# A state-space scan and a gated feed-forward layer on one core: first weights held, x on another queue, decay rows loaded once

## The chip, the cores and the metric

The kernel runs on one core of one Trainium2 chip. A core has a matrix engine (TensorE, PE in the profile), VectorE (DVE), ScalarE (ACT), GpSimd (POOL), SyncE (SP, which here only issues DMA transfers) and 16 DMA engines. Each engine works through its own instructions in order and waits on semaphores that other engines and transfers raise. The metric is the device time of one execution in microseconds (us); lower is better.

## The reference

Inputs: x (4 batches, 8 heads, 768 steps, 32 values), decay a (4, 8, 768), B and C (4, 8, 768, 16), all fp32, and two weight matrices in float64, w_in (256 x 2048) and w_out (2048 x 256). The first part is a Mamba-2 scan in chunks of 32 steps:

```python
log_a = np.log(np.clip(a, 1e-06, 1.0))
...
    cum = np.cumsum(la, axis=-1)
    L = np.exp(cum[:, :, :, None] - cum[:, :, None, :]) * causal
    y_intra = np.einsum('bhij,bhjd->bhid', (C_c @ B_c.T) * L, xc)
    y_inter = np.einsum('bhin,bhnd->bhid', Cc, state) * exp(cum)
    state = decay_full * state + sum over j of B_j x_j exp(cum_last - cum_j)
...
h = y @ w_in                 # y as (3072, 256)
g = h * (1.0 / (1.0 + np.exp(-1.702 * h)))
out = g @ w_out
```

(the middle lines are shortened; an einsum over heads and chunks is meant). The result is (3072, 256) fp32.

## The kernel before, in words

**Tiling.** The 768 steps are cut into NC = 6 chunks of 128, each of two halves of 64 steps. A group g holds one chunk of all four batches, 512 tokens; it has two pairs p of two batches each (PG = 2). For each group the scan gives yT (256 x 512), `hidden(g, f)` makes 16 blocks f of 128 hidden units from w_in, and a projection from w_out adds them up. For group 0 the products are plain (`hidden`, `project_all`); from group 1 on they use mixed operands with seven products for eight (`first`, `product`), which make up most of the span.

**Weights.** The float64 weights are fetched as 32-bit words in ten pieces (`PIECES`): 0 to 3 are 0.5 MB of w_in each (two blocks f), 4 and 5 are 1 MB of w_in each (four blocks), 6 to 9 are 1 MB of w_out each. `fetch(i)` issues the two transfers of piece i (line 175), on SyncE. Four buffers hold them, pieces 0 and 1 sharing one and 2 and 3 another, so pieces 6 to 9 are fetched when `join` of an earlier piece is done. With `held=True`, VectorE first writes one column of the target (line 166); since VectorE works in order, this holds the transfer, and all behind it on SyncE, until VectorE has come to that place.

A piece becomes fp32 in steps: `fields(i)` takes exponent and mantissa bits on VectorE (lines 188 and 191), `clamp(i)` does two Relu steps on ScalarE (200 and 202), `rounded(i)` adds the low word (206), `join(i)` sets the sign and multiplies (220 and 226), writing w_in or w_out. `narrow(i)` is rounded(i), fields(i+1), join(i), so join(i) stands behind the wait for piece i+1.

**The start.** Chunk 0 is done in its own way. a of chunk 0 (az0, four copies of 32 rows), C and B are loaded; VectorE turns C and B (`turn_blocks`, line 541); TensorE builds decay exponents in PSUM (493, 499, 488), ScalarE takes their exponential (529). GpSimd copies the decays to the ends (`drop_of`, 452) and scales C by the decay (`since_start`, 583). TensorE computes the scores C B (`score`, 597), VectorE multiplies the decays by them (`weigh`, 608) and B by the drops (`ends_first`, 458). `finish` multiplies by x (`intra`, 724) and by the state (`inter`, 709); `gain` (628) and `keep_first` (644) make the state; ScalarE copies yT (736). `pads` and `dense` are matmuls of ones with no use for the result, which fill places where TensorE would wait. Then `hidden(0, f)` runs for f = 0 to 15 (786), with other work hung in between by `at`.

**Queues around the change.** SyncE issues, in order: az0, half of C, part of B, piece 0, piece 1 (held until the first weighing), pieces 2 to 5 (held until after the ends), az, piece 6 and what follows. GpSimd issues the rest of B, builds `pick`, and issues x of pairs 0 and 1 (line 145) before its drops. az is all 768 steps of a, 32 rows written four times over into 128 partitions (line 1088); `clip` limits it on VectorE (361, 363) in `store_a`, which writes it to a DRAM scratch (1118); `pick_a` multiplies chunk 1 of it into operands on ScalarE (372).

`in_order` fixes the order of every engine's instructions to the program's.

## Time and profile before

| what | us |
|---|---|
| device time, three runs | 351.01, 353.86, 354.13; median 353.86 |
| profiled execution, device time | 352.01 |
| profiled execution, span | 350.3 |
| TensorE busy | 341.9 |
| VectorE busy | 255.8 |
| ScalarE busy | 149.5 |
| GpSimd busy | 40.7 |
| first block of `hidden(0, f)` starts | 17.42 |
| projection of group 0 starts | 49.0 |

The granted TensorE clock is full in every slice. The span runs from the first to the last instruction; the device time has 1.7 us around it. In the views, times are from the start of the span, "L608" is a line of the kernel, "x12" the number of instructions, and what stands in brackets is how long the engine was idle before and what ended that. Busy TensorE time is modelled from the starts of its instructions. DMA issues appear under the queue of their engine (SPq, POOL); the length there is that of issuing, not of the transfer.

### The profile page before, as it was taken

To read this page: it belongs to the slowest core of one execution; us is meant where nothing else is said; L and a number is where in the kernel's file an instruction comes from. 1 tells how busy PE (TensorE), PEld (TensorE's weight loads), DVE (VectorE), ACT (ScalarE), POOL (GpSimd) and SP (SyncE) were. 2 spreads that over 40 slices of the span, in tenths; PEclk is the share of its full clock that TensorE was granted. 3 is DMA by queue.
4 is the path that set the end of the run, shared out by engine and by line. 5 is a ranking of instruction groups with operands and counts; after the bars stand their busy time and mean duration, and the time that the engine had idled before them with its cause. 6 is when DMAs were issued, how large, how long until landed. Compare 5 with 4: busy or idle time off the path is not lost.

```text
span 350.3 us, 8534 instructions
## 1 busy us (share of the span) xinstructions
PE 341.9 (98%) x3514; PEld 281.1 (80%) x3514; DVE 255.8 (73%) x476; ACT 149.5 (43%) x333; POOL 40.7 (12%) x78
## 2 busy tenths in 40 slices
PE   8897999999999999999999999999999999999996
PEld 6666874545688888888888888888888888899996
DVE  7787999999789988749986557986454654455463
ACT  6767774005254322743442444433554321554320
POOL 8305500300297000000000000000000000000000
PEclk9999999999999999999999999999999999999999
DMA  5699986533529000466122326120000120000221
GB/s 136 187 296 253 279 180 148 87 72 59 94 57 189 2 0 5 74 129 100 23 35 60 52 78 120 21 33 9 0 4 2 17 33 12 1 2 0 33 31 60
DMA packets 82784, 26.02 MB, mean 74 GB/s; under 512 B 68841, under 2 KB 81001, under 8 KB 82745
## 3 DMA queue, kind: packets, MB, share of 16 engines
q1 hardware_dynamic: 79864, 23.41, 32.0%
q0 software_dynamic: 1888, 1.74, 2.2%
q8 instruction: 27, 0.44, 0.5%
q10 hardware_dynamic: 992, 0.33, 0.4%
q14 instruction: 13, 0.10, 0.1%
HBM read 22.22 MB, written 3.24 MB: 73 GB/s over the span
## 4 chain that ended last, share of the span: by engine, by line
PE 79%; DVE 8%; DMA 6%; POOL 3%; SPq 2%; issue 1%; ACT 1%; POOLq 0%; DVEq 0%
PE acc L944 28%; PE X L842 19%; PE Y L852 14%; PE acc L951 7%; DMA bits<-in_moe_w_out_dram 4%; PE y L724 3%; PE h L786 2%; PE y L709 2%; PE o L884 2%; DVE p L220 2%; SPq L269 1%; PE cb L597 1%; DMA a<-scratch 1%; DVE m L206 1%; DVE L L608 1%
## 5 line engine op out<-in xcount | busy, mean ns | idle before, releaser
L847 ACT ACTIVATE ac<-X 128x256 f32<-128x256 f32 x76 | 29.0, 382 | 80.0 <-PE X L842 79.6
L944 PE MATMUL acc<-mg,mw 128*128 128x256 f32 x192 | 54.5, 379 | 0.0
L971 DVE TENSOR_TENSOR gT<-Y,ac 128x512 f32<-128x512 f32 x38 | 26.2, 690 | 37.2 <-PE Y L852 33.9
L819 ACT ACTIVATE gT<-gT 128x512 f32<-128x512 f32 (+1 forms) x76 | 39.3, 519 | 31.7 <-DVE gT L971 31.1
L842 PE MATMUL X<-my,mi 128*128 128x256 f32 x152 | 45.1, 379 | 0.0
L971 DVE TENSOR_TENSOR gT<-Y,b 128x256 f32<-128x256 f32 x38 | 15.8, 418 | 34.0 <-PE Y L852 34.0
L944 PEld LDWEIGHTS acc<-mg,mw 128*128 128x128 f32 x192 | 36.5, 190 | 5.0
L786 PE MATMUL h<-yT,w_in 128*128 128x128 f32 (+2 forms) x182 | 36.3, 357 | 2.0 <-DVE w_in L226 1.8
L944 PE MATMUL acc<-gT,w_out 128*128 128x256 f32 x128 | 35.5, 379 | 0.0
L786 PEld LDWEIGHTS h<-yT,w_in 128*128 128x128 f32 x182 | 26.8, 191 | 10.3 <-issue 5.6
L842 PEld LDWEIGHTS X<-my,mi 128*128 128x128 f32 x152 | 28.0, 190 | 3.7
L884 PE MATMUL o<-gT,w_out 128*128 128x512 f32 x64 | 28.6, 597 | 0.0
L810 DVE TENSOR_TENSOR mg<-gT 128x512 f32<-128x512 f32 x40 | 27.2, 680 | 0.0
L944 PEld LDWEIGHTS acc<-gT,w_out 128*128 128x128 f32 x128 | 24.2, 190 | 3.4 <-ACT yT L759 0.2
L847 ACT ACTIVATE b<-X 128x256 f32<-128x256 f32 x38 | 14.6, 383 | 20.4 <-PE X L842 20.0
L842 PE MATMUL X<-yT,w_in 128*128 128x256 f32 x76 | 23.2, 389 | 0.0
L852 PE MATMUL Y<-yT,w_in 128*128 128x256 f32 x76 | 22.7, 381 | 0.0
L852 PE MATMUL Y<-my,mi 128*128 128x256 f32 x76 | 22.6, 379 | 0.0
L842 PE MATMUL X<-my,w_in 128*128 128x256 f32 x76 | 22.6, 381 | 0.0
L852 PE MATMUL Y<-yT,mi 128*128 128x256 f32 x76 | 22.5, 379 | 0.0
L884 PEld LDWEIGHTS o<-gT,w_out 128*128 128x128 f32 x64 | 11.8, 190 | 13.2 <-issue 12.7
L387 DVE TENSOR_TENSOR_SCAN L<-a,idents 128x1024 f32<-128x1024 f32 x9 | 20.5, 2274 | 0.0
(140 smaller groups left out, 569.3 us busy)
## 6 DMA issues: line engine op xcount, KB each, us to landing
a<-scratch SPq DMA_DIRECT2D x18, 256.0 KB
bits<-in_moe_w_out_dram SPq DMA_DIRECT2D x8, 512.0 KB
x<-in_x_dram SPq DMA_DIRECT2D x20, 128.0 KB
bits<-in_moe_w_in_dram SPq DMA_DIRECT2D x8, 256.0 KB
bits<-in_moe_w_in_dram SPq DMA_DIRECT2D x4, 512.0 KB
out_dram<-ob SPq DMA_DIRECT2D x128, 16.0 KB
af<-in_a_dram SPq DMA_DIRECT2D x20, 64.0 KB
zC<-in_C_dram SPq DMA_DIRECT2D x36, 32.0 KB
```

The costliest lines, as they stand in the source:

```text
L387: nc.vector.tensor_tensor_scan(out=L, data0=ra[p].rearrange("p k e -> p (k e)"), data1=idents.rearrange("p h i -> p (h i)"), initial=0.0, ...
L724: nc.tensor.matmul(out=y[i][t][D * q:D * q + D, 2 * n + k], lhsT=rx[p][side, k, h], rhs=L[side, k, h // Q, h % Q], start=begin(i, t, (q,)) ...
L786: nc.tensor.matmul(out=h[:, cols], lhsT=w_in[:, f, k], rhs=yT[g][:, k, cols], start=(k == 0 and e == 0), stop=(k == NK - 1), skip_group_ch ...
L810: nc.vector.tensor_tensor(out=t[:, 0:2], in0=B[:, :, 1], in1=B[:, 0], op=ALU.subtract)
L819: nc.scalar.activation(o, i, AF.Silu, scale=GELU_SCALE)
L842: nc.tensor.matmul(out=s["X"], lhsT=lhsT, rhs=rhs, start=i == "1", stop=i == "4", skip_group_check=True)
L847: nc.scalar.activation(copy, s["X"], AF.Copy)
L852: nc.tensor.matmul(out=o, lhsT=lhsT, rhs=rhs, start=s.pop("new", False), stop=i != "5", skip_group_check=True)
L884: nc.tensor.matmul(out=o[c], lhsT=w_out[:, c, f], rhs=gT[g, f // 2][:, f % 2], start=(f == 0), stop=(f == NF - 1), skip_group_check=True)
L944: nc.tensor.matmul(out=acc[g][0][i], lhsT=w, rhs=h, start=(j == 0 and (i, 0) in begins), stop=(j == NF // 2 - 1), skip_group_check=True)
L951: nc.tensor.matmul(out=o[k] if type(o) is list else o[:, cols], lhsT=h[:, cols], rhs=w, start=(j == 0 and (i, k) in begins), stop=(j == NF ...
L971: nc.vector.tensor_tensor(out=o, in0=v, in1=w, op=ALU.add)
```

## The change

Piece 0 is fetched after the turn of C, held by VectorE's memset, and x of both pairs follows it on SyncE instead of GpSimd. fields(0) (both steps) and clamp(0) come before the first weighing. a is loaded in two parts behind piece 1: chunk 1 in four copies (az1), and all chunks once, in 32 partitions (az); GpSimd clips both. One `dense` is left out and one comes a group earlier; there is one more pad.

```diff
-    az = ffn.tile([P, 4 * TG // 2], FP32, tag="mg", name="az", bufs=3)[:, :NC * P].rearrange(
+    az = ffn.tile([P, 4 * TG // 2], FP32, tag="mg", name="az", bufs=3)[:NB * NH, :NC * P].rearrange(
         "p (c s) -> p c s", c=NC)
+    az1 = const.tile([P, 1, P], FP32, name="az1")
...
     load_blocks(0, "B", [nc.gpsimd, nc.sync, nc.gpsimd, nc.sync, nc.gpsimd, nc.sync, nc.gpsimd, nc.gpsimd])
-    fetch(0)
...
-    for p in range(PG):
-        load(p, "x", nc.gpsimd)
...
     def clip(t):
 
-        nc.vector.tensor_scalar(out=t, in0=t, scalar1=1e-6, scalar2=1.0,
+        nc.gpsimd.tensor_scalar(out=t, in0=t, scalar1=1e-6, scalar2=1.0,
                                 op0=ALU.max, op1=ALU.min)
-        nc.vector.memset(t.rearrange(by_chunk, s=2)[:, :, :, 0], 0.0)
+        nc.gpsimd.memset(t.rearrange(by_chunk, s=2)[:, :, :, 0], 0.0)
...
         c, b = place(p)
+        assert c == 1
...
-                nc.scalar.activation(X[:, k, q], az[:, c], AF.Copy, scale=pick[:, b + k, q:q + 1])
+                nc.scalar.activation(X[:, k, q], az1[:, 0], AF.Copy, scale=pick[:, b + k, q:q + 1])
...
-                if p == 0 and (k, t) == (0, 1):
+                if p == 0 and (k, t) == (1, 0):
                     dense(begun_y["banks"][0][:, 2 * P:])
...
-            dense(begun_y["banks"][0][:, 2 * P:])
             intra(1, pairs[1])
...
-    pads(30, busy)
+    pads(31, busy)
...
     differ_of(0)
     turn_blocks(0, "C")
+    fetch(0, held=True)
+    for p in range(PG):
+        load(p, "x")
     mask_blocks(1)
...
     fold_ident(1)
+    fields(0)
+    clamp(0)
     weigh(0, (slice(0, 1),))
     fetch(1, held=True)
+    rows = a.rearrange("b h s -> (b h) s")
+    nc.sync.dma_start(out=az1[:, 0], in_=rows[:, P:2 * P].unsqueeze(0).to_broadcast([R, NB * NH, P]))
+    nc.sync.dma_start(out=az.rearrange("p c s -> p (c s)"), in_=rows)
+    for t in az1, az:
+        clip(t)
     weigh(0, (slice(1, 2),))
...
     for i in range(2, 6):
         fetch(i, held=i == 2)
-    nc.sync.dma_start(out=az.rearrange("p c s -> p (c s)"), in_=a.rearrange(
-        "b h s -> (b h) s").unsqueeze(0).to_broadcast([R, NB * NH, NC * P]))
-    fields(0, (0,))
     for k in range(2):
         weigh(1, (slice(k, k + 1),))
-    fields(0, (1,))
     rounded(0)
     finish(range(PG), (0,))
     gain(range(PG), (0,))
-    clamp(0)
     keep_first(0)
...
     def store_a():
-        clip(az)
         for i, side in enumerate(SIDES):
-            nc.sync.dma_start(out=scratch[:, i].rearrange("c r i -> r c i"), in_=az[:32, :, side])
+            nc.sync.dma_start(out=scratch[:, i].rearrange("c r i -> r c i"), in_=az[:, :, side])
```

## The prediction

> **What bounds the kernel now.** I read the page first, then the waits of the first 100 us, then the timeline of that part, then the DMA rows.

> The page: totals, and busy tenths in 40 slices of 8.76 us.

> ```profile
> span 350.3 us, 8534 instructions
> ...
> PE 341.9 (98%) x3514; PEld 281.1 (80%) x3514; DVE 255.8 (73%) x476; ACT 149.5 (43%) x333; POOL 40.7 (12%) x78
> ...
> PE   8897999999999999999999999999999999999996
> ...
> DVE  7787999999789988749986557986454654455463
> ...
> DMA  5699986533529000466122326120000120000221
> ```

> TensorE is the bound from slice 6 on: nothing the change touches can be gained there. What can move lies in the first four slices, where TensorE shows 8 and 7, and at places where it waits. Waits of 0 to 100 us (total, times, longest):

> ```profile
> DVE p L188 <- DMA bits<-in_moe_w_in_dram: 2.8, 2, 2.0
> ...
> PE h L786 <- DVE w_in L226: 1.8, 1, 1.8
> ...
> PE y L709 <- DVE L L608: 0.8, 1, 0.8
> DVE p L188 <- DMA bits<-in_moe_w_out_dram: 0.8, 1, 0.8
> ```

> So TensorE loses 1.8 us once to weights and 0.8 us once to a weighing, and VectorE waits on arriving weights. Timeline of 28 to 60 us (start, length, engine, line; idle before and its releaser):

> ```profile
> 31.31 0.69 DVE L188 TENSOR_SCALAR p<-bits 128x1024 uint32<-128x1024 uint32 x1 [2.00 <-DMA bits<-in_moe_w_in_dram]
> ...
> 34.08 3.69 PE L786 MATMUL h<-yT,w_in 128*128 128x256 f32 x16 [1.82 <-DVE w_in L226]
> ...
> 35.18 0.55 DVE L361 TENSOR_SCALAR az<-az 128x768 f32<-128x768 f32 x1
> ...
> 37.77 0.69 DVE L188 TENSOR_SCALAR p<-bits 128x1024 uint32<-128x1024 uint32 x1 [0.78 <-DMA bits<-in_moe_w_out_dram]
> ```

> Piece 5 of the weights lands at 31.3; join of piece 4, queued behind its fields, ends 2.6 later (33.93), and hidden block f=8 starts at 34.08 instead of 32.26. From 37.77, where piece 6 has landed, VectorE is busy 5.97 of each 6 us up to 62, and so on to the weighing that ends at 74.83: that stretch decides the 0.8. The start:

> ```profile
> 11.26 1.29 DVE L608 TENSOR_TENSOR L<-L,cb 128x512 f32<-128x512 f32 x2 [2.06 <-POOL CsT L583]
> ...
> 12.10 0.34 PE L724 MATMUL y<-L,x 64*32 64x64 f32 x16
> ...
> 12.89 0.70 PE L416 MATMUL y<-ones 128*128 128x256 f32 x2
> ...
> 14.44 0.70 PE L416 MATMUL y<-ones 128*128 128x256 f32 x2
> ...
> 17.42 8.88 PE L786 MATMUL h<-yT,w_in 128*128 128x512 f32 x30 [0.19 <-ACT yT L736]
> ```

> **The change, part by part.** *w0 held.* The memset waits for the turn of C (5.83 + 1.07 = 6.90), so SyncE issues fetch 0 at 7.0, not 5.36: 1.6 later. Its 0.52 MB went mostly in 6 to 9 us (168, 298 and 192 GB/s in those three microseconds). Shifted, it lands between 9.8 (8.0 plus 0.52 MB at 298) and 14.8 (13.15, its first use now, which shows no wait, plus 1.6). I take 10.7, from the rates.

> *fields(0) and clamp(0) ahead of the weighing.* VectorE is idle from 9.2 to 11.26, but now sits in order behind w0: fields (0.42 + 0.35) end at 11.5 and the first weighing starts 0.25 late (0 if w0 lands by 10.4; 4.3 late at the upper end). Behind that wait stand the weighings, both ends and the memsets that release fetch 1 and 2; TensorE's y and SyncE's queue wait for them. In return the two steps leave 13.15 (0.33 by the starts) and 14.68 (0.46): 0.79 less between weighing and first join. The two Relu steps (0.72 each) run at 12.04 to 13.5, in ScalarE's idle time, and keep_first no longer stands behind them.

> *x on SyncE.* GpSimd loses 3.55 us of issuing. It gains nothing at the weighing: after its x it already waits (0.17) for ScalarE's exponentials, which end at 10.52; drops and CsT stay where they are. SyncE gains four issues. x issues there later in the run take 0.37 to 2.76 us, median 0.59, so 7.97 + 2.35 = 10.3 (ends: 9.5 and 19.0). The packets shrink: around 49 us x runs at about 180 GB/s, so 0.52 MB take 2.9 us behind w0: the last lands at about 13.5. Now the last is issued at 9.29 and lands 4.6 later, 13.9. The gain needs it at about 14.0: no cost taken, 1.0 if it is 1 us late.

> *Dense and pads.* One dense (0.63) goes from before the second pair, where it is on TensorE's path since its weighing ends at 14.76. The other now stands before the second group instead of the third; it covers a wait of 0.16 there. One more pad (some 35 ns) ends before TensorE waits for the scan. Adding up from a weighing at 11.5: first group 12.35 to 12.7, dense 13.3, three groups 14.05, gain 14.6, second pair (its weighing ends at 14.9) 16.0, inter and copies 1.07: f=0 at 17.07, 0.35 earlier. This is paid back at once if f=8 still waits for piece 5.

> *a loaded once.* az1 and az are two more SyncE issues (some 0.47 each) between fetch 1 (12.3, now 12.0) and fetch 2 (14.1, now 13.27). Their 0.16 MB at the 235 GB/s of 13 to 16 us take 0.7. So pieces 2 to 5 move by +0.3 to +0.9. Gone is the old 0.39 MB. In the trace's packet records its 128 packets of 3072 bytes start between 25.5 and 32.6, about 20 per us at some 0.19 us each: four engines busy 6 us with it, ahead of piece 6 in the queue. Meanwhile throughput fell with all engines busy (clock, DMA share, GB/s at the end of each row):

> ```profile
> 22.00:26.00 4.00, 4.00 (x20) 3.43 (x19) 3.13 (x7) 2.69 (x5) 0.00 (x0) 1.00 1.10 367
> 26.00:32.00 6.00, 6.00 (x58) 4.97 (x56) 3.97 (x8) 3.79 (x6) 3.52 (x6) 1.00 1.12 248
> ```

> If az caused that fall, the 1.25 MB of those last 5 us would take 3.4 and piece 5 comes 1.6 sooner; if not, nothing comes back. With the shift: piece 5 moves by -1.3 to +0.9; I take -0.1, since its packets stand ahead of az in the queue. Piece 6 stands behind it and moves by about -3 to 0; I take -2.

> *Clip on GpSimd.* VectorE loses 0.55 + 0.07 at 35.18. GpSimd does 128 and 768 columns: by its memset of 512 (0.53) 0.9 us, by its multiply of 128 (0.44) 3.1. It needs to be done by 35.96, so its length is covered; it lies at about 16 to 19 beside VectorE's joins. The row for that: at 65 to 68.3, beside 3.29 us of GpSimd multiplies, two VectorE steps took 1.75 and 1.63 instead of 1.22 and 1.23, 0.93 us lost, 28%. So 0.25 to 0.9 us, 0.4 taken, and covered: the 0.8 and 2.0 us in which VectorE waits for pieces 4 and 5 take it up. Without those waits it would delay f=8 by as much.

> [...]

> *The sum.* f=8: 34.08 - 0.1 = 34.0, so TensorE reaches the weighing's wait 0.1 sooner (74.1). VectorE: ready for piece 6 at 36.99 - 0.62 - 0.1 = 36.3, piece 6 there at 35.7; everything to 74.83 comes 1.5 sooner, and the 0.79 wait disappears. Total 0.1 + 0.8 = 0.9 us. Profiled execution: 350.3 + 1.7 around it = 352.0; that gives 351.1. The median of the runs is 353.86, 1.85 above; the mean of the four executions is 352.75, which gives 351.8.

> **Rivals.** *Early weights.* If the fall was az's and w0 does not hold the weighing, TensorE gets the whole 1.82, the 0.79 and 0.35 to 0.6 of the start: 3.0 to 3.2 us, 349.6. For it: the fall coincides with the az packets. Against: piece 5 is queued ahead of them. The slower runs of 353.9 and 354.1 may hold longer waits of this kind, and then more is won.

> *Slower: x blocks SyncE.* At 41 to 43 us two x issues took 1.54 and 2.76, in a full queue; here they follow w0 in the same queue. At 2.15 each SyncE is free at 16.5, and every later piece is 4.5 late: f=8 at 38.6, all else as now, minus 0.8 at 74: 352.75 + 3.7 = 356.5. It decides from 1.0 us per issue ((12.0 - 7.97)/4). Against: 16 other x issues mostly took 0.6, and the queue holds only w0.

> *Nothing moves.* The weighing still starts by 11.3, pieces 5 and 6 arrive as now because the same 16 engines carry the same weights: 352.75.

> **How the numbers follow.** Forecast 0.45, early weights 0.25, x blocks 0.2, nothing 0.1. A measurement here tells about 1% (the three runs lie 0.9% apart). Early weights give 0.9%, more where waits were longer: 0.2 of its 0.25 counts as over 1%, with 0.07 of the forecast's upper end (piece 5 at -1.3: 2.1 us) when runs fall favourably. Faster 0.27, same 0.53 (0.38 + 0.05 + 0.1), slower 0.2. Range 349.0 to 356.0: early weights below, part of the blocked queue above, the ends of piece 5 (-2.1, +0.2) inside.

> **What would show it.** Right: first weighing at 11.3 to 11.8; f=0 near 17.1; no packets of az between 25 and 33; L188 of piece 6 without a wait; no wait before L709 at 74. Wrong: L188 of piece 0 waiting beyond 11.5 for DMA; x issues over 1 us on SyncE; L724 or L628 waiting for x; L188 of piece 1 waiting beyond 17.5; f=8 away from 34.0 by over 1.3 us.

## The result, and the profile after

The changed kernel takes 350.87 us (median of 18 runs, 349.66 to 352.79); the kernel before, run beside it, 353.79 us (18 runs, 351.01 to 355.53). The medians lie 2.9 us apart; the ratio of the runs is 0.9929, 95% interval 0.9910 to 0.9948, which is 2.5 us less. The forecast was 0.9 us less, 351.8 us, within a range of 349.0 to 356.0.

The profiled execution of the changed kernel took 352.79 us, the slowest of its 18; that of the kernel before had taken 352.01, faster than most of its own. Laid side by side, the two profiles say "0.8 us slower" where the runs say "2.5 us faster". Each has to be read for what happens in it, not for its end. The page of the changed kernel, totals and 40 slices:

```profile
span 351.1 us, 8536 instructions
...
PE   8799999999999999999999999999999999999996
...
DVE  7679998999879988648987457887464654455463
...
PEclk9769999999999999999999999999999999999999
DMA  3799995713529000367122427120000120000221
```

The row PEclk is new: in slices 2 and 3 TensorE was granted 0.7 and 0.6 of its clock, where every slice of before showed full. The stages (length; busy time and instructions of TensorE, its weight loads, VectorE, ScalarE, GpSimd; granted clock, DMA share, GB/s):

```profile
12.00:17.50 5.50, 3.84 (x138) 2.78 (x142) 5.16 (x13) 2.24 (x6) 0.12 (x1) 0.60 0.70 167
17.50:22.00 4.50, 4.50 (x67) 2.98 (x68) 2.60 (x7) 2.65 (x6) 2.75 (x3) 0.50 0.92 276
22.00:26.00 4.00, 4.00 (x9) 1.67 (x8) 3.93 (x8) 2.42 (x4) 1.32 (x2) 0.84 0.97 286
26.00:32.00 6.00, 6.00 (x58) 5.00 (x57) 5.93 (x12) 5.18 (x8) 1.36 (x2) 1.00 1.07 350
```

Two things stand in them: half clock from 13 to 23 us, and 350 GB/s at full share in 26 to 32, where before moved 248. Line numbers of the changed kernel lie one or two off those of before: its L189 is L188 there, L607 is L608, L708 is L709, L784 is L786. The start, in the timeline:

```profile
11.85 0.55 DVE L189 TENSOR_SCALAR p<-bits 128x512 uint32<-128x512 uint32 x1 [2.69 <-DMA bits<-in_moe_w_in_dram]
...
12.65 1.28 DVE L607 TENSOR_TENSOR L<-L,cb 128x512 f32<-128x512 f32 x2
...
13.37 0.47 PE L723 MATMUL y<-L,x 64*32 64x64 f32 x16 [2.10 <-DVE bits L167]
...
19.65 4.64 PE L784 MATMUL h<-yT,w_in 128*128 128x512 f32 x6
```

VectorE waits 2.69 us for piece 0, so the first weighing starts at 12.65 instead of 11.26; TensorE stands still for 2.1 us (11.27 to 13.37); the clock halves before that has ended (at 13.06); block f=0 starts at 19.65 instead of 17.42. The start became 2.2 us worse. And later:

```profile
30.84 8.90 PE L784 MATMUL h<-yT,w_in 128*128 128x256 f32 x40
...
31.38 0.69 DVE L189 TENSOR_SCALAR p<-bits 128x1024 uint32<-128x1024 uint32 x1
...
36.38 0.69 DVE L189 TENSOR_SCALAR p<-bits 128x1024 uint32<-128x1024 uint32 x1
```

None of these lines has a wait: the fields of pieces 5 (31.38) and 6 (36.38) find their weights landed, and TensorE runs through f=8 and, at 76 us, through line 708. By the chain of waits the span is now 95% TensorE, against 79% before. In these two executions the change lost 2.2 us at the start and won 1.4 behind it; that it wins more than it loses, only the medians say. What differs between kernels is made ahead of line 709 (708): from its start to the end of the span all 14 profiles of this document take 275.0 to 275.5 us.

### The profile page after: what moved, and what is told of

It is laid out like the page before. It is cut to its first block, busy times and chain, and to the rows that moved or that the text cites. A ratio compares the mean times of both kernels' runs of the same rounds, so it can differ in the third digit from the quotient of the medians.

```text
span 351.1 us, 8536 instructions
## 1 busy us (share of the span) xinstructions
PE 344.5 (98%) x3514; PEld 283.0 (81%) x3514; DVE 255.9 (73%) x475; ACT 149.3 (43%) x333; POOL 41.3 (12%) x78
## 3 DMA queue, kind: packets, MB, share of 16 engines
q0 software_dynamic: 1696, 1.22, 1.6%
## 4 chain that ended last, share of the span: by engine, by line
PE 95%; DMA 2%; DVE 1%; SPq 0%; issue 0%; ACT 0%; DVEq 0%
PE acc L942 28%; PE X L840 19%; PE Y L850 14%; PE h L784 11%; PE o L882 8%; PE acc L949 7%; PE y L723 3%; PE y L708 2%; PE cb L596 2%; DMA bits<-in_moe_w_in_dram 1%; PE A L627 1%; DMA zC<-in_C_dram 1%; DMA zB<-in_B_dram 0%; PE y L415 0%; DVE Ct L540 0%; PE y L627 0%
## 5 line engine op out<-in xcount | busy, mean ns | idle before, releaser
L845 ACT ACTIVATE ac<-X 128x256 f32<-128x256 f32 x76 | 29.1, 383 | 79.4 <-PE X L840 79.1
L784 PE MATMUL h<-yT,w_in 128*128 128x128 f32 (+2 forms) x182 | 37.9, 368 | 0.0
L784 PEld LDWEIGHTS h<-yT,w_in 128*128 128x128 f32 x182 | 27.6, 195 | 9.1 <-issue 6.7
L845 ACT ACTIVATE b<-X 128x256 f32<-128x256 f32 x38 | 14.6, 383 | 20.4 <-PE X L840 20.0
L882 PEld LDWEIGHTS o<-gT,w_out 128*128 128x128 f32 x64 | 11.8, 190 | 13.2 <-issue 12.9
```

The lines of the kernel that those rows point to most:

```text
L784: nc.tensor.matmul(out=h[:, cols], lhsT=w_in[:, f, k], rhs=yT[g][:, k, cols], start=(k == 0 and e == 0), stop=(k == NK - 1), skip_group_ch ...
L845: nc.scalar.activation(copy, s["X"], AF.Copy)
L882: nc.tensor.matmul(out=o[c], lhsT=w_out[:, c, f], rhs=gT[g, f // 2][:, f % 2], start=(f == 0), stop=(f == NF - 1), skip_group_check=True)
```

## The experiments

Theory A: what is won is won by the load of a. Theory S: it is won by the start (fields ahead, one dense less, x off GpSimd). Further runs take the start apart. Ratios are to the kernel before, run on the same chip with them.

### One part alone, and all but that part

`only_a` is the kernel before with a's loads and clip changed:

```diff
     fetch(1, held=True)
+    nc.sync.dma_start(out=az1[:, 0], in_=rows[:, P:2 * P].unsqueeze(0).to_broadcast([R, NB * NH, P]))
+    nc.sync.dma_start(out=az.rearrange("p c s -> p (c s)"), in_=rows)
+    for t in az1, az:
+        clip(t)                       # on GpSimd
...
-    nc.sync.dma_start(out=az..., in_=a...unsqueeze(0).to_broadcast([R, NB * NH, NC * P]))
```

> The kernel before with only the loads of a changed (az1 and az behind piece 1, clipped by GpSimd). Theory A, the gain is that of a's load: the throughput between 26 and 32 us stays above 330 GB/s instead of 248, pieces 5 and 6 land earlier, the 1.82 us wait of f=8 and the 0.79 us wait at 74 shrink; time 350.3 to 351.5, ratio to before 0.991 to 0.994. Theory S, the gain comes from the start (fields first, one dense less, x off GpSimd): 353 to 354, ratio 0.998 to 1.002.

`old_a` is the changed kernel with that diff reversed.

> The changed kernel with a loaded as before (four copies in one transfer behind piece 5, clipped by VectorE). Theory A: the fall of throughput is back, pieces 5 and 6 are late again, 353.5 to 355.5, ratio 0.999 to 1.005. Theory S: 351 to 352, ratio 0.992 to 0.995.

Measured: `only_a` 349.80 us, ratio 0.9919 (0.9888 to 0.9950); `old_a` 354.07, ratio 1.0025 (1.0000 to 1.0049). Theory A holds on both sides, and S falls: without a's loads all the rest of the change wins nothing, and with them alone the gain is there. `only_a`, stage 26 to 32 us and the fields of piece 6:

```profile
26.00:32.00 6.00, 5.25 (x50) 4.30 (x39) 5.67 (x10) 4.95 (x8) 2.79 (x5) 1.00 1.04 349
```

```profile
34.95 0.69 DVE L189 TENSOR_SCALAR p<-bits 128x1024 uint32<-128x1024 uint32 x1
```

`old_a`, waits of 4 to 100 us, of VectorE and TensorE:

```profile
DVE p L188 <- DMA bits<-in_moe_w_in_dram: 2.8, 2, 2.6
...
DVE p L188 <- DMA bits<-in_moe_w_out_dram: 2.5, 1, 2.5
...
PE y L722 <- DVE bits L166: 2.3, 1, 2.3
...
PE y L707 <- DVE L L606: 1.1, 1, 1.1
...
PE h L783 <- DVE w_in L226: 1.0, 1, 1.0
```

With the old load the waits for piece 6, at f=12 (43.06) and at the weighing (76.42) are back, and the late start (2.6, 2.3) comes on top. In `only_a` TensorE waits for weights once, 0.75 us at 29.04.

### The kernel before, once more

> The kernel before, once more, for a second profile. The median of its runs is 1.9 above its first profiled execution; if what differs is when pieces 5 and 6 land, the wait of f=8 is longer than 1.82 us here where the time is above 352, and everything before 25 us is as in the first profile to 0.3 us.

Measured: 353.04 us. Its timeline:

```profile
32.02 3.69 PE L786 MATMUL h<-yT,w_in 128*128 128x256 f32 x16 [0.23 <-DVE w_in L226]
...
38.61 0.69 DVE L188 TENSOR_SCALAR p<-bits 128x1024 uint32<-128x1024 uint32 x1 [3.26 <-DMA bits<-in_moe_w_out_dram]
42.46 3.81 PE L786 MATMUL h<-yT,w_in 128*128 128x128 f32 x32 [2.34 <-DVE w_in L226]
```

The expectation was wrong about the place. f=8 waits only 0.23 us here; piece 6 is the late one, VectorE waits 3.26 us for it, and TensorE 2.34 us at f=12, which the first profile did not show at all. With the wait at 74 (1.1) TensorE loses 3.7 us to late weights, where the first profile showed 2.6. The 0.75 of `only_a` is 2.9 less than 3.7, about what `only_a` wins.

### Why piece 6 is late: bytes or engines

`az_spread` is the kernel before with the same 0.39 MB in the same place, but as four transfers:

```diff
-    nc.sync.dma_start(out=az.rearrange("p c s -> p (c s)"), in_=a.rearrange(
-        "b h s -> (b h) s").unsqueeze(0).to_broadcast([R, NB * NH, NC * P]))
+    for r in range(R):
+        nc.sync.dma_start(out=az[32 * r:32 * r + 32].rearrange("p c s -> p (c s)"),
+                          in_=a.rearrange("b h s -> (b h) s"))
```

> The kernel before with its az load (0.39 MB, four copies, behind piece 5) issued as four transfers of 32 partitions, one per copy, in place of one transfer whose outermost dimension is the four copies. Theory E, the loss came from four engines carrying all of it: its 3072-byte packets are through within 3 us instead of 7, throughput in 26 to 32 us is above 310 GB/s, VectorE waits less than 1 us for piece 6, ratio 0.991 to 0.996 (350.5 to 352.2). Theory B, it came from the bytes, or from reading the same rows four times, in this place: throughput again near 245 GB/s, ratio 0.998 to 1.003.

Measured: 349.99 us, ratio 0.9902 (0.9882 to 0.9922). The stage, and the fields of piece 6:

```profile
26.00:32.00 6.00, 6.00 (x58) 4.97 (x56) 5.26 (x9) 5.27 (x8) 3.78 (x7) 1.00 1.10 265
```

```profile
35.35 0.69 DVE L188 TENSOR_SCALAR p<-bits 128x1024 uint32<-128x1024 uint32 x1
```

Theory E was right about piece 6, and the time came out a little below its range; it was wrong about the throughput: 265 GB/s, hardly more than the 248 of before, and the 3072-byte packets still start over 6 us (24.3 to 30.4). So the fall of throughput comes with this load, spread or not, and is not what costs. What costs is read from the semaphore records of the transfers, taken as one mark from every DMA engine that has finished its part of a transfer:

```
marks (us)                       before                         az_spread
az, each transfer                4, at 31.8 to 33.7             16, at 25.4 to 31.3
second half of piece 6           11 by 32.9, one at 35.0,       16, at 30.9 to 35.0
                                 the last four 36.0 to 37.7
```

By these marks four engines carry all of az in the kernel before. The last four marks of piece 6, which stands behind it, come 3 to 5 us after the eleven that were there by 32.9; we take them for the same four engines. Piece 6 is there with its last mark: at 37.7 us before (its fields start at 37.77, after a wait of 0.78), at 35.0 in `az_spread` and at 32.0 in `only_a`.

### The start: piece 0 held, fields ahead, x, dense

Four runs change the start of the changed kernel. `w0_free` issues piece 0 at its old place, unheld; `fields_late` puts fields(0) and clamp(0) back behind the weighings; `x_pool` and `x_first` are `fields_late` with x on GpSimd as before, or on SyncE ahead of piece 0.

```diff
 w0_free        (load_blocks B)  +    fetch(0)
                (turn_blocks C)  -    fetch(0, held=True)
 fields_late    -    fields(0); clamp(0)      (ahead of the first weighing)
                +    fields(0, (0,)) ahead of weigh(1), fields(0, (1,)) behind, clamp(0) behind gain
 x_pool         fields_late, and load(p, "x", nc.gpsimd) behind pick, none behind fetch(0)
 x_first        fields_late, and load(p, "x") behind pick, none behind fetch(0)
```

> The changed kernel with piece 0 issued unheld at its old place, x right behind it on SyncE. If holding w0 costs through the wait of fields(0) (2.69 us of VectorE in the changed profile) and the half clock behind it: fields(0) runs in VectorE's idle time, the first weighing starts at 11.1 to 11.4, the granted clock stays 1.0, f=0 at 16.6 to 17.1, time 349.3 to 350.3, ratio 0.987 to 0.990. If weights then bound f=8 again (DVE or piece 5), or the early w0 delays B: 350.5 to 351.2, ratio 0.991 to 0.993.

> The changed kernel with fields(0) and clamp(0) at their old places, between and behind the weighings of pair 1. If the wait of fields(0) costs: first weighing at 11.1 to 11.4, clock 1.0, f=0 at 17.0 to 17.6, time 349.8 to 350.6, ratio 0.988 to 0.991. If TensorE's lateness at the start is hidden by later waits for weights: as the changed kernel, 350.6 to 351.2, ratio 0.991 to 0.994.

> The changed kernel with fields(0) late (as in the run fields_late) and x issued by GpSimd at its old place; piece 0 still held. Theory H (holding piece 0 lets TensorE's next block of instructions load early, whatever queue x is on): scores without a gap, first weighing at 10.1 to 10.4; y no longer waits for x at 12.1 (1.12 in fields_late) and piece 1 lands by 16.5, so f=0 at 16.1 to 16.8; time 348.8 to 349.8, ratio 0.985 to 0.990. Rival, x on GpSimd is itself what delayed the instructions: the gap in the scores is back (0.5 to 1.2), first weighing at 11.0 to 11.3, f=0 at 16.9 to 17.3, 349.8 to 350.5.

> The changed kernel with fields(0) late and x issued by SyncE ahead of the held piece 0. If the queue order of x and piece 0 is what y waits for: y waits for no x, f=0 at 16.1 to 16.9, time 348.8 to 349.8, ratio 0.985 to 0.990. If x in the queue at 6 to 9 us delays TensorE's instructions as piece 0 did: a gap of 0.5 to 1.2 in the scores, f=0 at 17 or later, 349.8 to 350.8.

Measured: `w0_free` 349.83, ratio 0.9918 (0.9892 to 0.9944). `fields_late` 349.99, ratio 0.9915 (0.9882 to 0.9949); one of its six runs took 900.76 us, for which nothing here gives a cause. `x_pool` 352.03, ratio 0.9954 (0.9926 to 0.9982). `x_first` 350.15, ratio 0.9905 (0.9870 to 0.9941).

All four intervals hold the change's own 0.9929; times settle little here, and the profiles have to. `w0_free`, timeline of TensorE's scores:

```profile
9.14 0.94 PE L597 MATMUL cb<-CT,Bt 32*64 32x128 f32 x43
...
11.24 0.66 PE L597 MATMUL cb<-CT,Bt 32*64 32x128 f32 x21 [1.16 <-issue]
```

and in the changed kernel:

```profile
8.83 1.42 PE L596 MATMUL cb<-CT,Bt 32*64 32x128 f32 x64
```

The fields ran at 9.58 as expected, but the weighing started at 12.01, not 11.1: the scores broke off for 1.16 us, "issue", which waits for nothing that the profile shows. We take it that TensorE's instructions were missing. The page counts packets of the kind "instruction" beside those of the data (queue q8: 27 in a run, 0.44 MB, 0.5% of the 16 DMA engines' time); each is a block of 16 KB in the packet records, which show when the first one within the span starts:

```
kernel           piece 0   block starts (us)   gap in the scores (us)
before           unheld    8.2                 0.73
before_again     unheld    7.8                 none
only_a           unheld    7.9                 0.47
az_spread        unheld    8.0                 0.46
clip_dve         unheld    8.9                 1.29
w0_free          unheld    9.0                 1.16
after            held      7.1                 none
after_again      held      7.0                 none
fields_late      held      7.0                 none
x_pool, hold_a   held      7.4, 7.0            none
x_first          held      7.2                 0.26
old_a            held      7.0                 none
late_dense       held      7.0                 none
```

With piece 0 unheld its packets start at 6.0 to 6.5, ahead of the block; held, at 8.0 or later, behind it. Where there is a gap, the scores go on 1.3 to 1.8 us after the block is through, which is why we take it for the cause; whose instructions it holds, no record says. `x_pool` and `hold_a`, with x on GpSimd and no gap, bear out Theory H: it is piece 0, not the queue of x; the time of `x_pool` missed its forecast all the same (below). So holding piece 0 does have a use: in `fields_late` the first weighing starts at 10.12, where the two profiles of before have 11.26 and 10.98. What becomes of it, in that run's timeline:

```profile
10.12 1.30 DVE L607 TENSOR_TENSOR L<-L,cb 128x512 f32<-128x512 f32 x2 [0.98 <-PE cb L596]
...
12.15 0.35 PE L723 MATMUL y<-L,x 64*32 64x64 f32 x16 [1.12 <-DVE bits L167]
...
17.14 0.43 DVE L189 TENSOR_SCALAR p<-bits 128x512 uint32<-128x512 uint32 x1 [1.66 <-DMA bits<-in_moe_w_in_dram]
17.27 3.27 PE L784 MATMUL h<-yT,w_in 128*128 128x512 f32 x7 [0.19 <-ACT yT L735]
```

y comes 1.3 us after the end of its weighing (10.81), where before it came 0.15 after, though the engine named had long been done: x, behind piece 0 on the same queue, is the later input. Its first transfer is there at 12.02 (in `late_dense` below the same wait is put down to x). Piece 1, behind x, is then waited for too. In `x_first` f=0 starts at 16.79, the earliest of all, and it wins nothing that these runs can tell.

### The changed kernel once more, and its clock

> The changed kernel, once more. In its first profile (352.79, its slowest run) the granted clock was half from 13.5 to 23.5 us. In most runs the clock lies at 0.99 to 1.0; with a clock of 1.0 here, f=0 starts at 17.5 to 19, and the time is 350 to 351.

Measured: 351.75 us at a mean clock of 0.99, f=0 at 18.96; the wait of y is 2.2 us. Over the 18 runs, seven had a mean clock of 1.0 (median 350.60) and seven 0.99 or less (median 351.69): the half clock goes with about 1 us of a run, and eleven of the 18 have at least a little of it.

In the clock records of the traces the half clock lasts 10.24 us in the changed kernel (13.06 to 23.30) and in `late_dense` below, 6.83 us in this run (15.03 to 21.85) and 3.41 us in `old_a`: three, two and one times 3.41. The stretches at full clock keep to the same step: 327.68 us behind the fall in the changed kernel, 344.75 in the first profile of before, 96 and 101 times 3.41. The changed kernel in such steps, counted from where its clock changes, and below it two steps of `before_again`, which kept its clock (columns as in the stages above):

```profile
9.65:13.06 3.41, 1.62 (x34) 1.04 (x27) 1.22 (x3) 3.02 (x6) 1.50 (x4) 1.00 0.95 175
13.06:16.47 3.41, 3.10 (x104) 2.28 (x110) 3.41 (x10) 0.81 (x2) 0.00 (x0) 0.50 0.63 158
16.47:19.88 3.41, 3.12 (x107) 2.53 (x99) 2.27 (x7) 1.83 (x6) 0.75 (x1) 0.50 0.87 260
19.88:23.30 3.42, 3.42 (x5) 1.35 (x6) 2.31 (x5) 1.54 (x3) 3.24 (x3) 0.50 0.88 257
23.30:26.71 3.41, 3.41 (x12) 1.87 (x10) 3.34 (x9) 2.42 (x4) 0.08 (x1) 1.00 1.02 304
```

```profile
38.18:41.60 3.42, 1.94 (x18) 1.75 (x16) 2.95 (x4) 2.22 (x3) 2.94 (x5) 1.00 0.88 206
41.60:45.01 3.41, 2.55 (x23) 2.58 (x24) 3.41 (x6) 2.02 (x5) 0.00 (x0) 1.00 0.94 287
```

In the 14 profiles, ahead of the last matmuls, the clock fell behind the four steps in which TensorE was busy 1.10 to 1.71 us, and behind none with 1.94 or more. `before_again` stands still for 2.34 us at f=12, longer than the changed kernel's 2.1, but that is shared by two steps and the clock stays. So what goes with the fall in these traces is how much of a standstill lies in one step, and the steps begin at another place from run to run (one at 13.06 us in the changed kernel, at 15.03 in `after_again`, at 41.60 in `before_again`). What brings the clock back is not settled: it took one to three steps, in three of the four cases up to the end of the step in which `hidden` begins or which it fills.

### The dense, and the clip

`hold_a` is the kernel before with a's loads changed and piece 0 held, all else as before; from `x_pool` it differs in the dense and one pad. `late_dense` is `fields_late` with the removed dense back.

```diff
 hold_a      only_a, with  -    fetch(0)    (behind load_blocks B)
                           +    fetch(0, held=True)    (behind turn_blocks C)
 late_dense  fields_late, with  +            dense(begun_y["banks"][0][:, 2 * P:])    (ahead of intra(1, ...))
                                (k, t) == (0, 1), pads(30, busy)
 clip_dve    only_a, with clip on nc.vector, called for az1 and az in store_a
```

> The kernel before with a's loads changed and piece 0 held; x on GpSimd, dense, pads and the order of fields as before. It differs from x_pool in the dense and the pad alone. If the dense that was removed kept the clock up: clock 1.0 in most runs, 349.0 to 350.0, ratio 0.986 to 0.990. If x behind GpSimd with a held piece 0 is what costs in x_pool: clock 0.99 in half the runs or more, 351 to 352.5, ratio 0.994 to 0.998.

> The run fields_late with the removed dense back, the moved one at its old place, and 30 pads. If the dense is on TensorE's path at the start and the path reaches the end: 0.3 to 0.7 slower than fields_late, 350.2 to 350.8. If weights bound f=6 to f=8 anyway, or the dense keeps the clock at 1.0: as fields_late or up to 0.5 faster, 349.4 to 350.1.

> The run only_a with both clips on VectorE, in store_a as before (0.55 + 0.07 and some 0.3 for az1). If clipping on GpSimd wins what it takes off VectorE: 0.3 to 0.9 slower than only_a, 350.1 to 350.7, since VectorE's work behind piece 5 bounds later. If it is covered: within 0.3 of only_a, 349.5 to 350.1. [...]

Measured: `hold_a` 350.04, ratio 0.9911 (0.9890 to 0.9933). `late_dense` 352.95, ratio 0.9969 (0.9941 to 0.9997). `clip_dve` 350.41, ratio 0.9912 (0.9891 to 0.9934).

`hold_a` against `x_pool` says that the dense keeps the clock up: 0.99 in one of six runs, against eight of twelve. `late_dense` against `fields_late` says the opposite: with the dense, nine of twelve runs lie at 0.995 or below, without it one of six. Its profile:

```profile
12.72 0.35 PE L723 MATMUL y<-L,x 64*32 64x64 f32 x16 [1.35 <-DMA x<-in_x_dram]
```

```profile
12.00:17.50 5.50, 4.42 (x100) 2.78 (x100) 3.75 (x10) 2.35 (x6) 0.34 (x1) 0.64 0.88 206
```

Here the wait for x fell into one step (10.10 to 13.52) and left TensorE 1.71 us busy in it; the profile of `hold_a` has a standstill of 1.27 us that two steps share (2.60 and 2.66 busy), and the clock stayed. How often each kernel loses the clock these runs don't settle, and neither is the dense shown to matter. Runs at a mean clock of 0.99 lie 2 to 3 us above the others in `x_pool` (351.7 to 352.9 against 349.5 to 350.6), and much the same holds for `late_dense`.

`clip_dve` lies 0.6 us above `only_a`, but each ran beside its own runs of the kernel before, and the ratios are the same (0.9912 and 0.9919); its profile has the widest gap in the scores (1.29), which the clip has no part in. Not decided. What GpSimd needs for it is shown in the changed kernel: 0.75 us for 128 columns and 2.94 for 768, and the VectorE step beside its end (line 189 at 22.29) took 1.03 instead of 0.42.

## Why the prediction was right in its sign, and where it was short

**a loaded once: right in the mechanism, mis-sized.** The sum had 0.1 + 0.8 us for it; `only_a` measures 0.81%, 2.9 us. Two terms were small. Piece 6 was put at -2 us; it landed 4.4 us sooner in the changed kernel (33.3 against 37.7) and 5.7 in `only_a`. TensorE's gain behind it was limited to the 0.79 at 74: that rested on one execution, in which piece 6 came just in time for f=12. In `before_again` f=12 waits 2.34. The prediction had the median of the runs 1.85 above that execution and named longer waits as a possible reason, under a rival; it belonged into the sum.

**Partly luck.** The forecast of 351.8 lies only 0.9 above the median of 350.87, though the gain was 2.5 and not 0.9: it was counted from 352.75, the mean of four executions, where 18 runs of the kernel before have a median of 353.79. And a main term 2.0 us too small met a start that the sum took at nothing and that cost: `old_a` is 0.25% slower than before (interval 0 to 0.49%).

**"If az caused that fall": it did, and it hardly mattered.** Throughput went to 350 GB/s, but `az_spread` wins as much with 265. The row of packets, "four engines busy 6 us with it, ahead of piece 6", was the right one, and the prediction then used the other to size piece 5.

**Piece 5 at -0.1.** The changed kernel shows no wait for it, but TensorE comes to f=8 at 36.1 there, not 34.0, because of the start. Piece 5 landed at 30.4 instead of 31.2, but in `before_again`, with the old load, at 29.1: two executions of one kernel differ by more than the forecast move, and the 1.82 us at f=8 belonged to the first.

**fields(0) ahead of the weighing: the step that failed.** It said piece 0 lands at 10.7 and the weighing starts 0.25 late; it landed at 11.8 (11.2 in `after_again`) and the weighing started 1.4 late. The bounds (9.8 to 14.8) held it, the value taken was near the lower end. The rates of 6 to 9 us did not come again (228, 208 and 200 GB/s in 8 to 11 us, with x in them); SyncE's second issue now took 1.26 us instead of 0.47, and 14 of 16 engines were done by 11.2, the last at 11.8. Three of the prediction's own signs of being wrong are there: the fields of piece 0 wait beyond 11.5 (11.85), those of piece 1 beyond 17.5 (18.26), and f=8 is more than 1.3 off.

**f=0 at 17.07: wrong by 2.6 us**, 1.15 of it that weighing, most of the rest probably the half clock (from weighing to f=0 it is 7.0 us here, 6.4 in `after_again`, where the clock fell 2 us later, and 5.9 to 6.2 before), which the prediction did not consider: it took the rows' full clock for granted while adding a wait to TensorE. That is where the gain of 0.35 at the start went. It costs less at the end than at the place: f=0 starts 2.7 us later than in `only_a`, and the ratio differs by 0.1%, within the intervals.

**x on SyncE**: four issues, 8.67 to 12.07, 0.85 each: below the 1.0 at which the slower rival decides; the last x landed at 14.5 instead of 13.5, and in `fields_late` y waits for the first. *Nothing at the weighing from freeing GpSimd* was right, for its own reason; that the held piece 0 frees the scores was missed.

**Clip on GpSimd: about as forecast.** It took 0.75 and 2.94 us (0.9 and 3.1 were put down), and VectorE's steps beside it took 0.6 us longer in the changed kernel, 0 to 1.3 over the nine profiles with that clip (0.25 to 0.9 was the range, 0.4 taken). One or two steps were stretched each time; the others kept their length, such as lines 221 and 227 at 21.49 and 21.95 (0.42 us), beside the clip of 20.10 to 23.04.

**Rivals.** Early weights had the right load by the wrong way, the fall of throughput; without its start, which never came, its price of 1.82 + 0.79 = 2.6 us is near the 2.9 of `only_a`. The blocked SyncE did not happen. "Nothing moves" is excluded by the interval.

A plain version is `az_spread`: three lines on the kernel before. Its ratio of 0.9902 is better than the change's 0.9929, but the intervals overlap (0.9882 to 0.9922, 0.9910 to 0.9948), so it is not shown to be better.

## What to carry to other kernels

Ask of a transfer how many engines carry it, and what stands behind it on those engines: here a copy with an outermost dimension of four left four marks, and the last four marks of the piece behind it came 3 to 5 us late. Before sizing a wait from one profile, see where that execution lies among the runs; a wait that the profile shows as "just in time" may be the one that the median pays. And a wait that is moved onto TensorE's path may cost the clock on top of its length, here when it left TensorE busy for 1.62 us of a step of 3.41, and the half clock lasted 10.24 us.
